# A linear-attention and gated-MLP kernel: W_in through the hardware DMA queue, a halved first step, W_spatial transposed by DMA, filler matmuls and a new order

## The chip, the cores and the metric

The kernel runs on one core of a Trainium2 chip. The core has a matrix engine (PE, or TensorE; the profile lists its weight loads apart, as PEld), three other compute engines (DVE or VectorE, ACT or ScalarE, POOL or GpSimd) and a sync engine (SP) that here only issues DMAs. The metric is the device time of one execution in microseconds. Three timed executions of the kernel before gave 152.79, 153.34 and 153.37 us; the median is 153.34 us.

## The reference

Two layers follow each other. All inputs are float32; the output is float32 of 4 x 768 x 512.

1. Linear attention with decay, for 4 batches, 8 heads, 768 tokens and a head size of 64, in blocks of 64 tokens. For each block: `intra = ((q k^T) * decay mask) v`, `inter = (q * decay) state`, `out = intra + inter`, and then `state = lam^64 * state + (k * decay)^T v`. The heads are laid side by side, so the layer gives x of 768 x 512 per batch.
2. A gated MLP: `h = relu(x W_in)`, with W_in 512 x 1024; u is the first half of h, v the second; v is normalised over its 512 features; `v_s = W_spatial v_n + b` mixes tokens with a 768 x 768 matrix; the output is `(u * v_s) W_out`, with W_out 512 x 512.

## The kernel before

**Steps.** The work is cut into 12 steps n of 256 tokens, three to a batch. Token 2p+m of a step lies on partition p, in column group m. A step has these operations, each named by a short token with its step number:

- loads of q, k and v of the step, LQ, LK, LV (512 KB each, line 184, into three buffers of each kind, so that load n overwrites what load n-3 brought);
- KC and QC, casts to bfloat16 (lines 266 to 274); VD, v times its decay (line 292);
- TK and TQ, 8 PE transposes each (line 300), with EK and EQ, their evictions from PSUM (EQ multiplies by the decay, line 313);
- SC, scores (line 329), MK, their mask (line 333), KV, the state update (line 345), SS, a copy of the state, AV, intra and inter (lines 366 and 375), EX, the eviction of x to the tile xT;
- PV and EV, the v half of h and its relu (lines 401 and 406), BN, RA, RD, VN, the statistics and the normalisation; PU and EU, the u half (line 439).

When a batch's three steps are done, PW multiplies by the transposed W_spatial (line 461; f counts four blocks of features, i two halves of the 768 tokens), GB adds b (line 466), GM multiplies by u (line 472), PO multiplies by W_out (line 478; one block t of 128 output tokens), EO evicts and ST stores. GM for half i = 0 serves the PO blocks t = 0 to 2, half i = 1 the blocks 3 to 5. For the last four steps (8 to 11) q is scaled by QM, and the transposes of q and k are made by DMA (DQ, DK) instead of by the PE.

**Weights.** W_in, W_spatial and W_out are loaded by POOL through the software DMA queue, which casts float32 to bfloat16 on the way (WI, WS, WO, lines 239 to 248). In front of each stands GT (line 235), a copy of one element of a named q, k or v buffer: POOL waits there until the load that last wrote this buffer has landed, so the weight is not requested earlier. W_spatial is transposed by the PE (WT, 72 matmuls, line 451) and evicted by DVE and ACT (EW). WT takes every second column, which brings the tokens into the order of the partitions; GM (line 472) then reads u with a stride to bring the result back to token order.

**Order.** The order is written out by hand in a string, `ORDER`. Each token is operation, numbers, engine (T for PE, A for ACT, D for DVE, P for POOL, S for SP). Every engine runs its own tokens strictly in this order, and waits where an input or a buffer is not ready; a DMA that must wait also holds back all that stands behind it on its queue. Dependences follow from the order of the tokens: an operation that reads a buffer waits for the last token before it that writes that buffer.

Of the kernel before, what the change touches and what calls it, by code (L numbers as in the profile page):

```python
# [16 lines left out]
LK.0.2.S lam.A msk.P LQ.0.2.S LK.1.2.S idn.P mkc.D LV.0.2.S LB.6.T pos.P LN.6.A LK.2.2.S LL.D KC.0.2.P LX.A  # L17
LQ.1.2.S TK.0.6.T LT.0.A QC.0.2.D LQ.2.2.S TQ.0.5.T EK.0.6.A EQ.0.5.D KC.1.2.A SC.0.0.0.T LV.1.2.S SC.0.1.2.T
LT.2.A MK.0.0.0.D TK.1.6.T VD.0.2.P EK.1.6.A MK.0.1.2.D LV.2.2.S LT.1.A AV.0.0.0.T LK.3.2.S KV.0.0.T SS.0.0.A
GT.1.1.P WI.0.P QC.1.2.D KV.0.1.T AV.0.1.0.T KC.2.2.A LQ.3.2.S GT.1.1.P WI.1.P TQ.1.6.T EX.0.1.1.A TK.2.5.T  # L20
EQ.1.6.D GT.1.2.P WS.1.P EX.0.0.0.A QC.2.2.D EK.2.5.A SC.1.0.2.T LQ.4.2.S GT.1.2.P WS.0.P SC.1.1.0.T
MK.1.0.2.D TQ.2.6.T SS.0.1.A VD.1.2.P EQ.2.6.D MK.1.1.0.D SC.2.0.2.T SC.2.1.4.T MK.2.0.2.D AV.1.0.0.T KV.1.0.T
LV.3.2.S MK.2.1.4.D SS.1.0.A KV.1.1.T VD.2.2.P AV.1.1.0.T SS.1.1.A PV.0.0.6.T EX.1.1.1.A EX.1.0.0.A PV.0.1.1.T
EV.0.0.6.A AV.2.0.2.T BN.0.0.D PV.1.1.6.T EV.0.1.1.D KV.2.0.T BN.0.1.D PV.1.0.5.T SS.2.0.A EV.1.1.6.D RA.0.A
AV.2.1.2.T BN.1.1.D PU.1.0.6.T BS.S EV.1.0.5.A RD.0.D PU.0.1.4.T VN.0.0.D EX.2.1.3.A KC.3.2.P BN.1.0.D
EX.2.0.2.A PU.1.1.5.T EU.0.1.4.A EU.1.0.6.D PV.2.0.3.T RA.1.A VN.0.1.D EU.1.1.5.A RD.1.D TK.3.6.T VN.1.1.D
EV.2.0.3.A PU.2.0.2.T VN.1.0.D EK.3.6.A BN.2.0.D PV.2.1.3.T EU.2.0.2.A PU.2.1.6.T EV.2.1.3.A LK.4.2.S WT.3.2.T
BN.2.1.D EU.2.1.6.A QC.3.2.P WT.4.3.T WT.0.5.T EW.3.2.D RA.2.A WT.1.6.T LK.5.2.S EW.4.3.D EW.0.5.A WT.5.4.T
WT.2.2.T RD.2.D VN.2.1.D EW.5.4.A TQ.3.3.T QC.4.2.P VN.2.0.D PU.0.0.5.T EW.2.2.A EQ.3.3.D LQ.6.2.S EW.1.6.A
TQ.4.4.T VD.3.2.P SC.3.1.0.T EU.0.0.5.A EQ.4.4.D SC.3.0.2.T PW.0.0.1.6.T LQ.5.2.S MK.3.1.0.D PW.0.1.1.5.T  # L30
GB.0.0.1.6.D LV.4.2.S MK.3.0.2.D PW.0.1.0.4.T GM.0.0.1.P KC.4.2.A PW.0.0.0.6.T GB.0.1.1.5.D GB.0.1.0.4.D
LK.6.2.S GM.0.1.1.P TK.4.5.T GB.0.0.0.6.D PW.0.2.1.4.T GM.0.1.0.P EK.4.5.D LK.7.2.S AV.3.0.0.T GT.0.5.P WO.P
GB.0.2.1.4.D SC.4.0.2.T SC.4.1.5.T KV.3.0.T MK.4.0.2.D PW.0.3.1.4.T GM.0.2.1.P SS.3.0.A LV.6.2.S QC.6.2.P
MK.4.1.5.D KV.3.1.T AV.3.1.0.T KC.5.2.A PW.0.3.0.3.T GM.0.0.0.P SS.3.1.D GB.0.3.1.4.D LV.5.2.S QC.5.2.A
TK.5.6.T EX.3.1.1.D GM.0.3.1.P PW.0.2.0.2.T GB.0.3.0.3.D EX.3.0.0.A VD.4.2.P EK.5.6.A GM.0.3.0.D TQ.5.3.T
GB.0.2.0.2.D PV.3.1.5.T EQ.5.3.D PU.3.0.6.T EV.3.1.5.A GM.0.2.0.P AV.4.0.0.T BN.3.1.D EU.3.0.6.A SC.5.1.2.T
SC.5.0.4.T LQ.8.2.S KV.4.0.T MK.5.1.2.D PV.3.0.6.T SS.4.0.A MK.5.0.4.D KV.4.1.T EV.3.0.6.A AV.4.1.0.T LK.8.2.S
KC.6.2.P PO.0.0.3.T EX.4.0.0.A BN.3.0.D EX.4.1.1.A PO.0.1.6.T EO.0.0.3.D RA.3.A LK.9.2.S PV.4.0.2.T RD.3.D
SS.4.1.D EO.0.1.6.A VN.3.1.D VD.6.2.P VN.3.0.D PV.4.1.3.T EV.4.0.2.A ST.0.0.S TK.6.6.T BN.4.0.D EV.4.1.3.A
PO.0.2.2.T EK.6.6.A BN.4.1.D VD.5.2.P TQ.6.3.T LV.9.2.S EO.0.2.2.A PU.3.1.5.T EQ.6.3.D RA.4.A PO.0.3.6.T  # L40
QM.8.0.D QM.8.1.P EU.3.1.5.A ST.0.1.S RD.4.D AV.5.0.0.T VN.4.1.D EO.0.3.6.A SC.6.0.2.T VN.4.0.D SC.6.1.4.T
KV.5.0.T MK.6.0.2.D PO.0.5.6.T SS.5.0.A KC.7.2.P ST.0.3.S AV.5.1.0.T MK.6.1.4.D LQ.11.2.S TK.7.3.T EX.5.1.1.A
PU.4.0.2.T EX.5.0.0.A EK.7.3.A PV.5.1.5.T LK.10.2.S EU.4.0.2.A PV.5.0.4.T ST.0.2.S EV.5.1.5.A LQ.7.2.S
PU.5.1.3.T EO.0.5.6.A BN.5.1.D EV.5.0.4.A PO.0.4.6.T EU.5.1.3.A BN.5.0.D ST.0.5.S PU.5.0.2.T EO.0.4.6.A
LV.8.2.S RA.5.A PU.4.1.3.T EU.5.0.2.A RD.5.D VN.5.0.D AV.6.0.0.T VN.5.1.D EU.4.1.3.A KV.6.0.T ST.0.4.S
PW.1.0.0.6.T SS.6.0.A PW.1.0.1.5.T GB.1.0.0.6.D LQ.9.2.S GM.1.0.0.P PW.1.1.0.6.T GB.1.0.1.5.D LV.7.2.S
QC.7.2.D GM.1.0.1.P KV.6.1.T AV.6.1.0.T GB.1.1.0.6.D KC.8.2.A PW.1.2.0.5.T EX.6.0.0.D DQ.8.S GM.1.1.0.P
EX.6.1.1.A SS.6.1.D PW.1.2.1.6.T DK.8.S GB.1.2.0.5.D VD.8.2.P PW.1.3.0.5.T GB.1.2.1.6.D LK.11.2.S PU.6.0.6.T
GB.1.3.0.5.D GM.1.2.0.P TQ.7.4.T GM.1.3.0.D EU.6.0.6.A GM.1.2.1.P PU.6.1.5.T EQ.7.4.D LV.11.2.S QM.9.0.P
PO.1.0.6.T EU.6.1.5.A SC.7.0.0.T VD.7.2.P EO.1.0.6.A SC.7.1.2.T PO.1.2.5.T MK.7.0.0.D LQ.10.2.S PV.6.1.6.T  # L50
MK.7.1.2.D QM.9.1.P PO.1.1.4.T LV.10.2.S EV.6.1.6.A EO.1.2.5.D AV.7.0.0.T BN.6.1.D EO.1.1.4.A SC.8.1.2.T
SC.8.0.5.T KV.7.0.T MK.8.1.2.D PV.6.0.4.T ST.1.1.S SS.7.0.A KV.7.1.T MK.8.0.5.D EV.6.0.4.A AV.7.1.0.T
PW.1.1.1.3.T SS.7.1.A ST.1.0.S VD.9.2.P EX.7.1.1.D AV.8.0.4.T EX.7.0.0.D GB.1.1.1.3.D KV.8.0.T DQ.9.S
PU.7.1.6.T KC.9.2.D SS.8.0.A GM.1.1.1.P KC.10.2.A BN.6.0.D AV.8.1.4.T QM.10.1.P PV.7.0.3.T EU.7.1.6.A DK.9.S
QM.10.0.D EX.8.0.4.A DK.10.S PV.7.1.6.T RA.6.A VD.10.2.P EV.7.0.3.A RD.6.D VN.6.1.D DQ.10.S EX.8.1.5.A
PW.1.3.1.2.T BN.7.0.D PV.8.1.3.T EV.7.1.6.D GB.1.3.1.2.D PV.8.0.6.T ST.1.2.S EV.8.1.3.A BN.7.1.D GM.1.3.1.P
PU.7.0.2.T EV.8.0.6.A BN.8.1.D QM.11.0.P RA.7.A PO.1.3.3.T BN.8.0.D EU.7.0.2.A QM.11.1.P PO.1.5.6.T VN.6.0.D
EO.1.3.3.A RD.7.D RA.8.A VN.7.1.D SC.9.0.0.T ST.1.3.S EO.1.5.6.A SC.9.1.2.T VN.7.0.D PO.1.4.5.T MK.9.1.2.D
ST.1.5.S PU.8.1.6.T EO.1.4.5.A RD.8.D MK.9.0.0.D PU.8.0.4.T ST.1.4.S EU.8.1.6.A VN.8.0.D AV.9.0.0.T EU.8.0.4.A
VN.8.1.D SC.10.1.2.T SC.10.0.5.T KV.9.0.T MK.10.1.2.D PW.2.0.0.4.T SS.9.0.A MK.10.0.5.D KV.9.1.T AV.9.1.0.T  # L60
KC.11.2.A PW.2.1.0.3.T DQ.11.S VD.11.2.P GB.2.0.0.4.D SS.9.1.D EX.9.0.0.A DK.11.S PW.2.1.1.6.T GB.2.1.0.3.D
EX.9.1.1.A PV.9.0.5.T GM.2.0.0.P GB.2.1.1.6.D PU.9.1.4.T GM.2.1.1.P EV.9.0.5.A PV.9.1.6.T BN.9.0.D GM.2.1.0.P
EU.9.1.4.A PW.2.3.1.5.T EV.9.1.6.A BN.9.1.D PW.2.3.0.6.T GB.2.3.1.5.D RA.9.A AV.10.0.0.T GB.2.3.0.6.D
GM.2.3.1.P SC.11.0.2.T SC.11.1.4.T RD.9.D KV.10.0.T MK.11.0.2.D PU.9.0.6.T SS.10.0.A VN.9.1.D KV.10.1.T
# [12 lines left out]
"""


@with_exitstack  # L80
def kernel(
    ctx: ExitStack,
    tc: tile.TileContext,
    q: bass.AP,
    k: bass.AP,
    v: bass.AP,
    lam: bass.AP,
    moe_w_in: bass.AP,
# [6 lines left out]
    P = 128  # L95
# [158 lines left out]
    def ld_k(e, n, x):  # L254
        load(k, k_in, n, *hx(x), e)
# [47 lines left out]
    def t_k(e, n, b):  # L303
        tr(n, b, kc)
# [230 lines left out]
```

## Time and profile before

| | |
|---|---|
| median of the timed runs | 153.34 us |
| time of the profiled execution | 152.98 us |
| its span, first to last instruction | 151.2 us |
| PE busy | 133.6 us, 88% |
| DVE / ACT / POOL busy | 106.9 / 81.4 / 75.6 us |
| DMA | 30.73 MB, mean 203 GB/s |

The profile is one execution. A busy time is a sum over instructions, a span is a time on the clock; the busy shares of the engines overlap. Durations of single matmuls overlap each other, so the time that a group of matmuls takes is read from the chain of work that ended last, where each piece has the time that it added. "x8" behind a piece is its number of instructions.

### The profile page before, as it was taken

The numbers are of one execution on the slowest core, as the hardware profiler recorded it, in microseconds if no ns is written. First come the engines' busy times: TensorE is split into PE (matmuls) and PEld (weight loads), VectorE is DVE, ScalarE is ACT, GpSimd is POOL, SyncE is SP. The second block draws the span as 40 slices with busy tenths as digits, with TensorE's granted clock in tenths as the row PEclk, the third lists the DMA queues.
The fourth block names the chain that finished last, engine by engine and source line by source line (L and its number), as shares of the span: only waits on it lengthen the run. The fifth ranks groups of instructions, "written<-read, shape, count | busy, mean of one in ns | idle before, by whom it ended". The sixth has DMA issues, their size and how long they took to land.

```text
span 151.2 us, 4756 instructions
## 1 busy us (share of the span) xinstructions
PE 133.6 (88%) x2026; PEld 87.2 (58%) x2026; DVE 106.9 (71%) x190; ACT 81.4 (54%) x146; POOL 75.6 (50%) x74
## 2 busy tenths in 40 slices
PE   1274947999999989977999999999999999999990
PEld 1264844677766754645766756556657655666540
DVE  1454593986999998685747799999958981936701
ACT  3987815698623837737724434765553344831161
POOL 7425980203669922780039975990293240016520
PEclk9999999999999999999999999999999999999999
DMA  3999999999988998999999799994170003121255
GB/s 108 300 290 290 283 216 216 217 248 304 281 221 237 172 301 216 269 310 342 319 341 276 142 306 311 202 208 177 41 138 4 2 4 139 57 81 72 74 219 197
DMA packets 52040, 30.73 MB, mean 203 GB/s; under 512 B 9522, under 2 KB 48946, under 8 KB 52018
## 3 DMA queue, kind: packets, MB, share of 16 engines
q1 hardware_dynamic: 49488, 27.53, 71.0%
q0 software_dynamic: 2384, 2.75, 10.6%
q8 instruction: 16, 0.26, 0.7%
q10 hardware_dynamic: 146, 0.13, 0.3%
q14 instruction: 6, 0.05, 0.1%
HBM read 24.77 MB, written 6.29 MB: 205 GB/s over the span
## 4 chain that ended last, share of the span: by engine, by line
PE 70%; DMA 16%; DVE 5%; SPq 4%; issue 2%; POOL 0%; ACT 0%; ACTq 0%
PE ps L461 20%; PE ps L439 13%; PE ps L401 13%; PE ps L478 11%; DMA q_in<-in_q_dram 10%; DMA win_sb<-in_moe_w_in_dram 6%; SPq L184 4%; PE ps L375 3%; PE ps L345 3%; PE ps L329 3%; PE ps L300 2%; PE ps L366 2%; PE ps L451 1%; DVE vsb L466 1%; DVE vn L430 1%
## 5 line engine op out<-in xcount | busy, mean ns | idle before, releaser
L472 POOL TENSOR_TENSOR gT<-vsb,uT 128x384 bf16<-128x384 f32 x27 | 30.1, 1128 | 33.6 <-DVE vsb L466 33.3
L461 PE MATMUL ps<-wt_sb,vn 128*128 128x384 bf16 x192 | 33.9, 327 | 0.0
L292 POOL TENSOR_TENSOR vd<-v_in,lv 128x1024 bf16<-128x1024 f32 x12 | 22.8, 1905 | 17.1 <-issue 6.4
L333 DVE TENSOR_TENSOR a_sb<-ps,m 128x1024 bf16<-128x1024 f32 x24 | 28.4, 1214 | 1.8 <-PE ps L329 1.6
L416 DVE BATCH_NORM_STATS2 st<-vh 128x6 f32<-128x512 bf16 x24 | 16.5, 688 | 11.9 <-ACT vh L406 11.7
L461 PEld LDWEIGHTS <-vn 128*128 128x128 bf16 x192 | 17.9, 98 | 11.9
L401 PE MATMUL ps<-win_sb,xT 128*128 128x512 bf16 x96 | 23.6, 380 | 0.8 <-DMA win_sb<-in_moe_w_in_dram 0.8
L439 PE MATMUL ps<-xT,win_sb 128*128 128x256 bf16 x192 | 24.1, 273 | 0.0
L478 PE MATMUL ps<-wout_sb,gT 128*128 128x512 bf16 x96 | 23.4, 380 | 0.0
L466 DVE TENSOR_TENSOR vsb<-ps,bsp 128x384 f32<-128x384 f32 x32 | 17.6, 552 | 6.8 <-PE ps L461 5.4
L439 PEld LDWEIGHTS <-win_sb 128*128 128x128 bf16 x192 | 18.3, 98 | 4.4
L168 ACT ACTIVATE o_sb<-ps 128x512 f32<-128x512 f32 (+1 forms) x21 | 12.3, 586 | 14.9 <-PE ps L478 10.7
L406 ACT ACTIVATE vh<-ps 128x512 bf16<-128x512 f32 x21 | 12.5, 597 | 13.6 <-PE ps L401 13.6
L406 ACT ACTIVATE uT<-ps 128x512 bf16<-128x512 f32 x22 | 13.2, 598 | 6.9 <-PE ps L439 6.7
L401 PEld LDWEIGHTS <-xT 128*128 128x128 bf16 x96 | 8.8, 98 | 9.6 <-issue 0.8
L478 PEld LDWEIGHTS <-gT 128*128 128x128 bf16 x96 | 9.0, 98 | 8.8
L168 ACT ACTIVATE s_sb<-ps 128x256 bf16<-128x256 f32 x14 | 5.3, 381 | 16.1 <-PE ps L345 16.1
L430 DVE TENSOR_SCALAR vn<-vh,mv,rstd 128x512 bf16<-128x512 bf16 x24 | 12.5, 551 | 0.3
L375 PE MATMUL ps<-a_sb,vd 64*64 64x128 bf16 x384 | 11.1, 225 | 1.7 <-DVE a_sb L333 1.0
L168 ACT ACTIVATE kc<-k_in 128x1024 bf16<-128x1024 f32 x7 | 7.4, 1056 | 8.4 <-PE ps L345 5.1
L168 ACT ACTIVATE xT<-ps 128x512 bf16<-128x512 f32 x19 | 10.5, 591 | 1.4 <-PE ps L375 1.3
L329 PE MATMUL ps<-qT,kT 64*64 64x128 bf16 x384 | 8.4, 233 | 2.5 <-DVE qT L313 2.5
(64 smaller groups left out, 155.6 us busy)
## 6 DMA issues: line engine op xcount, KB each, us to landing
k_in<-in_k_dram SPq DMA_DIRECT2D x12, 512.0 KB, 7.3
q_in<-in_q_dram SPq DMA_DIRECT2D x12, 512.0 KB, 7.3
v_in<-in_v_dram SPq DMA_DIRECT2D x12, 512.0 KB, 7.1
out_dram<-o_sb SPq DMA_DIRECT2D x23, 256.0 KB, 2.5
wsp_raw<-in_moe_w_spatial_dram POOLq DMA_DIRECT2D x2, 576.0 KB, 16.1
win_sb<-in_moe_w_in_dram POOLq DMA_DIRECT2D x2, 512.0 KB, 10.6
wout_sb<-in_moe_w_out_dram POOLq DMA_DIRECT2D x1, 512.0 KB, 10.7
bsp<-in_moe_b_spatial_dram SPq DMA_DIRECT2D x1, 384.0 KB, 8.1
```

The costliest lines, as they stand in the source:

```text
L168: nc.scalar.activation(out=o, in_=i, func=AF.Copy)
L292: vec(e).tensor_tensor(out=vd[n % NCA][:, h], in0=v_in[n % NIN][:, h], in1=lv[:, n % NR, h].unsqueeze(3).broadcast_to((P, h.stop - h.start ...
L333: nc.vector.tensor_tensor(out=a_sb[n % NA][:, i].rearrange("p o w j x -> p (o w) (j x)"), in0=bank(b, 2).rearrange("p o (w y) -> p (o w) y ...
L375: nc.tensor.matmul(out=po[row(w), c ^ o, c, i], lhsT=vd[n % NCA][row(c), 4 * o + u, j, :], rhs=a[row(c), i, o, w, j, :], start=(r == 0 and ...
L401: nc.tensor.matmul(out=bank(b), lhsT=x[:, c, g], rhs=win_sb[:, g, DH:DFF], start=(g == 0), stop=(g == NCH - 1))
L406: nc.scalar.activation(out=o, in_=i, func=AF.Relu)
L416: nc.vector.bn_stats(out=st6[p2][:, t], in_=vh[p2][:, t])
L439: nc.tensor.matmul(out=pu[:, f2].rearrange("p (c x) -> p c x", c=2), lhsT=win_sb[:, g, f * P:(f + 1) * P], rhs=x[:, :, g, :], start=(g == ...
L461: nc.tensor.matmul(out=bank(b)[:, 0:HW], lhsT=vn[bb % 2][:, s, f * P:(f + 1) * P], rhs=wt_sb[:, s, i * HW:(i + 1) * HW], start=(s == 0), s ...
L466: nc.vector.tensor_tensor(out=vsb[(bb * 4 + f) % NVS][:, i * HW:(i + 1) * HW], in0=bank(b)[:, 0:HW], in1=bsp[:, i * HW:(i + 1) * HW], op=A ...
L472: vec(e).tensor_tensor(out=gT[bb % 2][:, f, cols].rearrange("p (a y m) -> p a y m", m=2, y=Q64), in0=vsb[(bb * 4 + f) % NVS][:, cols].rear ...
L478: nc.tensor.matmul(out=bank(b), lhsT=gT[bb % 2][:, f, t * P:(t + 1) * P], rhs=wout_sb[:, f, :], start=(f == 0), stop=(f == NCH - 1))
```

## The change

- **W_in** is loaded in float32 by SP, through the hardware queue: WI.0 (the v half, 1 MB) into the output buffer o_sb, which is idle then and is now one tile, WI.1 (the u half) into a new tile wst. New operations WC cast it, one of four row blocks each (two on ACT, two on DVE, four on POOL).
- **Step 0** is loaded, cast, transposed and scored in halves of four heads each; a half is two DMAs of 128 KB. VD works in halves in all steps.
- **W_spatial** stays on the software queue, but is transposed by six DMAs on SP (DW, each a block of 128 x 768, SBUF to SBUF). WT and EW go. The token order is now set where AV writes PSUM (a strided output), and GM reads and writes contiguous rows.
- **Fillers**: WU issues matmuls of 128 x 128 on a constant, 136 in all, 105 of them ahead of the first PV.
- VN runs on ACT for 16 of its 24 tiles (as `rstd * v - mean * rstd`, so RD makes a second small tile, nmr). SY, a copy of two elements, stands in front of nine EX pairs. Step 8's q and k are transposed by the PE again; DQ and DK remain for steps 9 to 11.
- **A new order.** The whole string is new. On SP it begins Q0 and K0 in halves, Q1, K1, V0 in halves, V1, WI.0, Q2, K2, WI.1, V2, K3, Q3, V3, K4, Q4, K5, V4, Q5, Q6, b, V5, DW.0, DW.1, DW.2, K6, Q7, V6, K7, DW.4, DW.3, DW.5, V7, ST.0.2, Q8. On POOL it holds ... VD.3.1, VD.3.0, GT.2.0, WS.0, KC.5, VD.4.1, VD.4.0, QC.5, VD.5.0, GT.2.2, WS.1, GT.0.3, WO, GM.0.1.0, KC.6, GM.0.3.0, QC.7, GM.0.2.0. On the PE, the four PW of batch 0 with i = 0 stand behind all of steps 0 to 4, and the first PO behind all of step 5.

```diff
-LK.0.2.S lam.A msk.P LQ.0.2.S LK.1.2.S idn.P mkc.D LV.0.2.S LB.6.T pos.P LN.6.A LK.2.2.S LL.D KC.0.2.P LX.A
...
+LQ.0.1.S lam.A pos.P LK.0.1.S LQ.0.0.S LK.0.0.S msk.P WU.-8.T LB.1.T LQ.1.2.S LN.1.A LL.D idn.P LK.1.2.S
+QC.0.1.A LX.A LV.0.1.S KC.0.1.D WU.15.T TQ.0.1.2.T LT.0.A TK.0.1.0.T LV.0.0.S QC.0.0.D WU.4.T TQ.0.0.6.T
...
+SC.5.1.3.T BN.3.0.D LK.6.2.S SC.5.0.1.T PV.4.1.5.T EU.4.1.6.A MK.5.0.1.D VD.5.0.P VN.1.0.A LQ.7.2.S PU.3.0.0.T
+VD.5.1.D EV.4.1.5.A GT.2.2.P WS.1.P PU.4.0.6.T VN.2.1.A MK.5.1.3.D LV.6.2.S GT.0.3.P WO.P TQ.6.1.T EU.4.0.6.A
...
     def load(src, dst, n, x, e):
+        if x == 2:
+            eng.dma_start(out=dst[n % NIN].rearrange("p h m d -> p h (m d)"),
+                          in_=src[b, :, t].rearrange("h (p m) d -> p h (m d)", m=2))
+        else:
+            for h in (2 * x, 4 + 2 * x):
+                eng.dma_start(out=dst[n % NIN][:, h:h + 2].rearrange("p h m d -> p h (m d)"),
+                              in_=src[b, h:h + 2, t].rearrange("h (p m) d -> p h (m d)", m=2))
...
+    def w_u(e, n):
+        if n < 0:
+            nc.vector.memset(warm, 1.0)
+        for x in range(abs(n)):
+            nc.tensor.matmul(out=bank(SB)[:, 4 * D:4 * D + P], lhsT=warm, rhs=warm, start=(n < 0 and x == 0), stop=True,
+                             skip_group_check=True)
...
     def after(e, x, n):
-        nc.gpsimd.tensor_copy(out=seen, in_=(k_in, q_in, v_in)[x][n % NIN][0:1, 0, 0, 0:1])
+        nc.gpsimd.tensor_copy(out=seen[:, 0:1], in_=(k_in, q_in, v_in)[x][n % NIN][0:1, H - 1, 0, 0:1])
 
     def w_in(e, j):
         f = slice(DH, DFF) if j == 0 else slice(0, DH)
-        nc.gpsimd.dma_start(out=win_sb[:, :, f],
-                            in_=moe_w_in.rearrange("(g p) f -> p g f", p=P)[:, :, f])
+        nc.sync.dma_start(out=stage(j), in_=moe_w_in.rearrange("(g p) f -> p g f", p=P)[:, :, f])
+
+    def stage(j):
+        return o_sb[:, 0:NCH] if j == 0 else wst
+
+    def w_c(e, j, g):
+        f = slice(DH, DFF) if j == 0 else slice(0, DH)
+        copy(e, win_sb[:, g, f], stage(j)[:, g])
...
     def a_v(e, n, part, b):
-        po = bank(b, 2).rearrange("p z (c i x) -> p z c i x", c=2, i=2)
+        po = bank(b, 2).rearrange("p z (c i y m) -> p z c i m y", c=2, i=2, m=2)
...
+    def s_y(e, n, b):
+        copy(e, seen, ps[0:1, b:b + 2, 0:1].rearrange("p z x -> p (z x)"))
...
     def v_n(e, n, c):
         t, p2 = 2 * (n % NR) + c, n // NR % 2
+        if e == "A":
+            nc.scalar.activation(out=vn[p2][:, t], in_=vh[p2][:, t], func=AF.Identity,
+                                 scale=rstd[p2][:, t:t + 1], bias=nmr[p2][:, t:t + 1])
+            return
...
-    def w_t(e, s, b):
-        pw = bank(b).bitcast(BF16)
-        for a in range(NT):
-            for m in range(2):
-                nc.tensor.transpose(out=pw[row(m), a * P:(a + 1) * P], in_=wsp_raw[:, a, s * P + m:(s + 1) * P:2],
-                                    identity=ident)
-
-    def e_w(e, s, b):
-        pw = bank(b).bitcast(BF16)[:, 0:S]
-        copy(e, wt_sb[:, s], pw)
+    def d_w(e, a):
+        nc.sync.dma_start_transpose(wt_sb[:, :, a * P:(a + 1) * P], wsp_raw[:, a])
...
-        vec(e).tensor_tensor(out=gT[bb % 2][:, f, cols].rearrange("p (a y m) -> p a y m", m=2, y=Q64),
-                             in0=vsb[(bb * 4 + f) % NVS][:, cols].rearrange("p (a y m) -> p a y m", m=2, y=Q64),
-                             in1=uT[bb % 2][:, f, cols].rearrange("p (a m y) -> p a y m", m=2, y=Q64), op=ALU.mult)
+        vec(e).tensor_tensor(out=gT[bb % 2][:, f, cols], in0=vsb[(bb * 4 + f) % NVS][:, cols],
+                             in1=uT[bb % 2][:, f, cols], op=ALU.mult)
```

## The prediction

> **What bounds the kernel now.** I read the busy time by stage first, with cuts where the chain of work changes hands: the first PV (24.00), the first PW (40.25), the first PO (57.13), the end of the last PE wait (69.30), the last matmul (147.50). Columns: stretch, its length, busy time of PE, PEld, DVE, ACT, POOL, granted clock, DMA share, GB/s.
>
> ```profile
> 0.00:24.00 24.00, 12.67 (x299) 10.67 (x300) 12.70 (x19) 16.16 (x30) 14.72 (x24) 1.00 1.08 246
> 24.00:40.25 16.25, 16.25 (x265) 11.61 (x264) 12.07 (x28) 12.37 (x22) 4.18 (x4) 1.00 1.13 252
> 40.25:57.13 16.88, 16.15 (x312) 10.70 (x305) 16.32 (x22) 7.08 (x11) 12.07 (x12) 1.00 0.99 238
> 57.13:69.30 12.17, 10.34 (x160) 6.30 (x158) 9.74 (x19) 7.35 (x14) 7.29 (x5) 1.00 1.03 273
> 69.30:147.50 78.20, 78.20 (x1007) 47.95 (x1004) 55.67 (x104) 38.01 (x70) 37.30 (x30) 1.00 0.63 162
> ```
>
> From 69.30 on the PE never stops. Ahead of that the DMA is full, and the PE waits for data. The chain that ended last (start, duration, what) names the waits:
>
> ```profile
> 14.00 0.65 POOL seen L235
> 14.65 9.29 DMA win_sb<-in_moe_w_in_dram
> 23.94 0.04 issue
> 23.98 1.89 PE ps L401 x8
> ...
> 57.49 7.18 DMA q_in<-in_q_dram
> 64.67 0.02 issue
> 64.69 0.88 DVE qc L277
> ...
> 67.67 1.14 DVE a_sb L333
> 68.81 0.04 issue
> 68.85 0.61 PE ps L300 x8
> ...
> 142.33 5.19 PE ps L478 x24
> ```
>
> W_in is asked for only at 14.65 and the PE gets it at 23.94. A late q load, then a full DVE, hold the PE before 68.85. The queues and weight loads, from the page (queue: packets, MB, share of 16 engines; load: count, KB, median us from issue to landing):
>
> ```profile
> q1 hardware_dynamic: 49488, 27.53, 71.0%
> q0 software_dynamic: 2384, 2.75, 10.6%
> ...
> wsp_raw<-in_moe_w_spatial_dram POOLq DMA_DIRECT2D x2, 576.0 KB, 16.1
> win_sb<-in_moe_w_in_dram POOLq DMA_DIRECT2D x2, 512.0 KB, 10.6
> wout_sb<-in_moe_w_out_dram POOLq DMA_DIRECT2D x1, 512.0 KB, 10.7
> ```
>
> So the time is: when does the PE become saturated, and how much work has it left then.
>
> **The PE's work.** Prices from the chain, per token: PV and PO 0.865 (x8 in 1.73), PU 0.87, PW 1.01, a pair of SC 0.50, AV 0.46 (0.22 where a batch begins), KV 0.24, TK and TQ 0.45, all WT 2.13. Counted over the PE's tokens: 125.2 before, 124.0 after (WT goes; step 8's two transposes come, 0.9). Check: from 69.30 to 147.50 these prices give 77.1 for 78.2, so a remainder is multiplied by 1.014. Behind the last matmul lie 3.7 of span (the same halves EH and SH stay), and 1.8 outside the span (152.98 against 151.2). In the new order the work ahead of a token is: first PV 5.7, first PU 10.5, KV.3.0 16.6, KV.4.0 23.0, TQ.5 27.0, KV.5.0 32.8, first PW 33.5, first PO 42.3.
>
> **When data lands.** Loads before landed at 4.9, 6.7, 8.5, 10.4, 12.2, 14.0, 15.8: 1.8 per 512 KB while the hardware queue is alone. Step 0's eight half DMAs are issue-bound (0.5 each on SP against 0.45 of transfer): K0 lands at 7.1 instead of 6.7. Then Q1 8.9, K1 10.7, V0 12.5, V1 14.3. W_in's 1 MB halves have no row: at the rate of these loads 3.6; the best slice of the page, 342 GB/s, mixes loads with stores whose rows are 2 KB as W_in's are, and if stores were half of it they ran at 415 GB/s, 2.5. I take 2.8, nearer the rows of equal length. So WI.0 17.1, Q2 18.9, K2 20.7, WI.1 23.5, V2 25.3, K3 27.1, Q3 28.9, V3 30.7, K4 32.5, Q4 34.3, K5 36.1, V4 37.9.
>
> WS.0 stands on POOL behind VD.3 (two halves at about 1.0; a full VD is 1.9, and a 512-element QM 1.05 in the median), so it is issued at 32.9. Software loads landed 9.3 (the first W_in) to 17.5 after issue, the long ones behind others; alone I take 10: 42.9. It also takes engine time from the hardware queue: 10.6% of 151.2 is 16.0 for 2.75 MB, so 3.4 for its 0.59 MB. Hence Q5 43.1, Q6 44.9, b 46.3, V5 48.1.
>
> **The walk, part by part.**
>
> *Start.* PV.0.0 needs WI.0 and a cast (half of a 1.04 POOL cast, 0.53): 17.7. The PE is there at about 18.0, after VD.1 (16.3) and AV.1. Before it was 23.98, with 1.4 more of step 2 done. The 105 fillers ahead of PV.0.0 (0.056 each when transposes run at x8 in 0.45, so 5.9) lie in PE waits for step 0 and 1's loads; uncovered they would cost those 5.9. SP loses nothing: WI is issued while the queue is full anyway.
>
> *Second half of W_in.* WI.1 at 23.5 and three POOL casts in a row: PU.0.0 at 25.1 (W 10.5). WC on DVE, ACT (0.35 to 0.6 each) delay EQ.2 and QC.2, which wait for step 2's loads longer.
>
> *Steps 2 to 4.* KV.3.0: 25.1 + 6.1 + 0.8 for 15 fillers is 32.0, VD.3 is ready at 32.7. KV.4.0: 39.1, VD.4 ready at 39.9. TQ.5: 43.9, QC.5 ready at 44.1. KV.5.0 at 49.9; VD.5 was ready at 49.1.
>
> *W_spatial by DMA.* DW.0 waits on SP for WS.0 (42.9). K6, Q7, V6 and K7 queue behind it. A transpose of 128x1024 held SP for 1.24 to 2.77 and landed after 3.1 to 4.0; a block has three quarters of that. Price of one block in the queue: from 0.9 to 3.6; I take 1.2, three quarters of the median issue (1.6). Behind V5: 48.1 + 3.6 = 51.7. The PE reaches the first PW at 50.6 and waits 1.1. EW's 3.9 of ACT and DVE goes.
>
> *W_out.* GT.0.3 reads a k buffer whose last writer in the new order is K6, no longer K3. K6 lands at 53.5, POOL holds WO until then, and GM.0.1.0, KC.6 and QC.7 behind it. WO is issued at 53.7 and lands 9.3 to 11.9 later. I take 9.3: SP stands at DW.4 for WS.1 (49.3 + 10), so the hardware queue runs dry. That is 63.0. The PE reaches the first PO at 51.7 + 8.8 = 60.5 and waits 2.5.
>
> *Rest.* DW.3 to 5 are done near 63 + 1, and V7, ST.0.2, Q8 behind them by 70; their users stand 8 or more later (PW.0.0.1 at 63.0 + 5.9, TQ.8 at 79). No wait counted.
>
> *Costed at nothing.* VN on ACT: 16 of about 0.6, 9.6 on an engine with 70 idle; DVE loses 8.8 of its 106.9, and it was full from 40 to 57. Identity is not in the trace: if it needed table loads (1.28 each, up to two for each of 12 RA), 30 of ACT, which at 54% would still be beside PE mostly; I take 0. AV's strided output: nearest row is WT's strided weight load, 110 ns against 98; from 0 to a doubling of AV, 10; I take 0, and below nothing is excluded since the matmuls are the same. GM contiguous: DVE 1.22 to perhaps 0.55 (the row of GB), five of them, not on the path after 69. SY: 9 of 0.1 to 0.2. POOL: about 3 more of VD and WC in halves against 75.6.
>
> **Sum.** 63.0 + 1.014 x 81.7 (82.8) + 3.7 + 1.8 = 151.3, against 152.98: minus 1.7. On the median of 153.34 that is 151.6; I say 151.5.
>
> **A rule against the row.** Moving W_in between queues is spoken against by the Trainium skill, "DMA: Bandwidth & Descriptors", section "Issuing engines are not separate DMA queues": DMAs of all issuers run on the same 16 engines, and another issuer saves only issue time. The trace agrees on the sharing: K3 took 14.6 to land beside the software loads, 7.3 is the usual. By that rule alone W_in costs the same 7.2 for 2 MB at the loads' rate and the sum would be 1.6 later; what I count is its earlier request, not bandwidth. The same page, "Latency and other measured facts", has DMA transposes at 261 GB/s: 0.75 for a block, an estimate, so WO and the sum would be 1.4 earlier. No run here shows that rate.
>
> **The rivals.**
>
> *A, the weights are hidden (0.27).* GT.0.3 or the transposes cost less, and the first PO starts when the PE gets there without either wait: 59.4. Then 59.4 + 82.8 + 3.7 + 1.8 + 0.36 (to the median) = 148.1. For it: W_out before landed at 56.7, just ahead of its PO. Against it: K6 behind three transposes.
>
> *B, slower: the transposes clog SP's queue (0.25).* One mechanism: DW blocks cost more than 1.2. At 2.4, K6 and so WO are 3.6 later: 155.2; at 3.6 it is 158.8. It decides when W_out lands after 64.7, that is at 1.8 per block. For it: landings of 3.1 to 4.0 each, a median SP hold of 1.76 for qT. Against it: that row has full-size transposes and several waits on other work.
>
> *C, no net change (0.08).* W_in ahead of steps 2 to 5 only moves the wait: DMA is full to 69 either way, and the 6 gained at the first PV are lost to later loads. 153.3.
>
> *Forecast (0.40):* its own range 150 to 153.
>
> **Numbers.** The measurement can tell about 0.5% (0.8 us) from no change. Faster: A and four fifths of the forecast, 0.59. Same: C and 0.05 of the forecast, 0.13. Slower: B and what is left, 0.28. The range of 8 in 10 runs from 146.5 (A with the KV waits gone too) to 157.0 (B at 3 per block).
>
> **What would show it.** Right: first PV (matmul group of win_sb with xT) near 18, first PU near 25, first PW near 52, a PE wait at the first PO that ends with the DMA of wout_sb near 63, no PE wait after 70; POOL's `seen` ended by k_in near 53. Wrong: the PE waiting for wt_sb for many us (B), no wait at the first PO (A), DVE or ACT as releaser of PE waits between 30 and 60, AV pieces longer than 0.46, or ACT table loads beside the first three.

## The result and the profile after

The changed kernel takes 158.99 us (median of four runs, 157.34 to 159.53) against 153.3 us for the kernel before on the same chip: a ratio of 1.036, 95% interval 1.028 to 1.044. The forecast was 151.5, a gain, in a range from 146.5 to 157.0; the kernel became slower instead. The profiled execution after took 159.53 us; its span is 157.8 (before: 152.98 and 151.2). Ratios, here and below, leave out executions that are more than 1.5% above the fastest of the same kernel, and medians do not, so where the two disagree both are given.

The parts of the page after that answer to those shown of before: busy time (share of the span, instructions), the granted TensorE clock in 40 slices, the queues (packets, MB, share of 16 DMA engines) and the share of the chain that ended last by engine.

```profile
span 157.8 us, 4968 instructions
PE 148.6 (94%) x2106; PEld 100.5 (64%) x2106; DVE 98.6 (62%) x191; ACT 92.7 (59%) x171; POOL 68.5 (43%) x83
PEclk9999995999999999999999999999999999999998
q1 hardware_dynamic: 53376, 30.28, 77.5%
q0 software_dynamic: 1328, 1.70, 6.1%
PE 87%; DMA 5%; SPq 3%; ACT 2%; issue 1%; DVE 0%; ACTq 0%; DVEq 0%
```

TensorE (PE) is busy for 148.6 us, 15.0 more than before (133.6), though the count of work tokens says that it has 1.2 us less to do. The chain that ended last is PE for 87% (before: 70%), DMA for only 5% (before: 16%). So the waits that the change was to remove did go, and the time came out longer: the work itself has become dearer. The fillers are in the 15.0 (136 of them, busy 13.4 in the modelled ends; those ahead of the first PV lie mostly where the PE would have stood idle, as run e3 below shows). The rest is found by setting the same pieces of the chain (start, duration, what) beside each other. First before, then after:

```profile
25.87 0.24 PE ps L366 x8
26.11 0.22 PE ps L375 x16
```

```profile
34.37 0.34 PE ps L414 x8
34.72 0.44 PE ps L423 x16
```

These are the two kinds of matmul of AV (L366 and L414: q with the state; L375 and L423: the masked scores with v). The reader is to see that 16 matmuls of the same shape take 0.44 in place of 0.22, and 8 take 0.34 in place of 0.24. The group in the page says it again, busy time and mean ns behind the bar, before and after:

```profile
L375 PE MATMUL ps<-a_sb,vd 64*64 64x128 bf16 x384 | 11.1, 225 | 1.7 <-DVE a_sb L333 1.0
```

```profile
L423 PE MATMUL ps<-a_sb,vd 64*64 64x128 bf16 x384 | 16.1, 310 | 0.0
```

The stretches by 1 us of the kernel after (columns as in the prediction) show a second, small loss: the PE stands for most of 23 to 24 with no releaser, and then runs at half clock for 3.4 us, over its first PV.

```profile
22.00:23.00 1.00, 0.77 (x36) 0.66 (x24) 0.00 (x0) 0.97 (x2) 0.41 (x1) 1.00 1.02 373
23.00:24.00 1.00, 0.12 (x4) 0.13 (x4) 0.00 (x0) 0.23 (x1) 0.63 (x1) 0.96 1.06 367
24.00:25.00 1.00, 1.00 (x7) 0.39 (x6) 0.00 (x0) 0.00 (x0) 0.00 (x0) 0.50 1.17 311
25.00:26.00 1.00, 1.00 (x5) 0.45 (x4) 0.00 (x0) 0.00 (x0) 0.00 (x0) 0.50 1.21 295
26.00:27.00 1.00, 1.00 (x13) 1.00 (x11) 0.00 (x0) 0.96 (x2) 0.91 (x2) 0.50 1.23 286
27.00:28.00 1.00, 1.00 (x9) 0.65 (x8) 0.42 (x1) 0.41 (x2) 0.82 (x3) 0.83 1.13 281
```

From the stop at 22.8 to the end there is no PE wait above 0.2, none for W_out among them, although the rest of the forecast's chain is in place (K6 landed at 55.3, W_out was issued at 55.73 and landed at 64.9): the PE, slowed by AV, reaches the first PO only at 68.78. In the other three executions of this kernel the mean granted clock was 0.995 to 1.00 (0.987 in this one), and they took 157.34 to 159.09, so the half clock does not explain the loss.

### The profile page after: what moved, and what is told of

The parts are those of the page before. It is cut to its first block, busy times and chain, and to the rows that moved or that the text cites. A ratio compares the mean times of both kernels' runs of the same rounds, so it can differ in the third digit from the quotient of the medians.

```text
span 157.8 us, 4968 instructions
## 1 busy us (share of the span) xinstructions
PE 148.6 (94%) x2106; PEld 100.5 (64%) x2106; DVE 98.6 (62%) x191; ACT 92.7 (59%) x171; POOL 68.5 (43%) x83
## 4 chain that ended last, share of the span: by engine, by line
PE 87%; DMA 5%; SPq 3%; ACT 2%; issue 1%; DVE 0%; ACTq 0%; DVEq 0%
PE ps L512 20%; PE ps L452 14%; PE ps L498 14%; PE ps L528 13%; PE ps L423 7%; PE ps L336 5%; DMA k_in<-in_k_dram 5%; PE ps L414 4%; PE ps L377 4%; PE ps L393 3%; PE ps L214 3%; SPq L197 2%; ACT kc L176 1%; ACT s_sb L176 0%; SPq L193 0%
## 5 line engine op out<-in xcount | busy, mean ns | idle before, releaser
L523 POOL TENSOR_TENSOR gT<-vsb,uT 128x384 bf16<-128x384 f32 x27 | 24.4, 912 | 43.0 <-DVE vsb L517 42.8
L322 POOL TENSOR_TENSOR vd<-v_in,lv 128x512 bf16<-128x512 f32 x23 | 23.9, 1055 | 9.3 <-DMA v_in<-in_v_dram 7.6
L452 PE MATMUL ps<-win_sb,xT 128*128 128x512 bf16 x96 | 25.3, 391 | 0.0
L423 PE MATMUL ps<-a_sb,vd 64*64 64x128 bf16 x384 | 16.1, 310 | 0.0
L176 ACT ACTIVATE xT<-ps 128x512 bf16<-128x512 f32 x21 | 11.8, 595 | 7.0 <-PE ps L423 7.0
L214 PE MATMUL ps<-warm 128*128 128x128 bf16 x136 | 13.4, 255 | 2.1 <-DVE warm L212 1.1
L457 ACT ACTIVATE uT<-ps 128x512 bf16<-128x512 f32 x20 | 11.9, 593 | 4.3 <-PE ps L498 4.3
L486 ACT ACTIVATE vn<-vh,nmr,rstd 128x512 bf16<-128x512 bf16 x16 | 12.9, 812 | 2.5 <-DVE nmr L480 2.5
L362 DVE TENSOR_TENSOR qT<-ps,lq 128x1024 bf16<-128x1024 bf16 (+1 forms) x10 | 6.4, 636 | 12.7 <-ACT s_sb L176 7.5
L214 PEld LDWEIGHTS <-warm 128*128 128x128 bf16 x136 | 10.7, 116 | 4.0 <-issue 1.9
## 6 DMA issues: line engine op xcount, KB each, us to landing
wst<-in_moe_w_in_dram SPq DMA_DIRECT2D x1, 1024.0 KB, 10.7
```

The lines of the kernel that those rows point to most:

```text
L176: nc.scalar.activation(out=o, in_=i, func=AF.Copy)
L214: nc.tensor.matmul(out=bank(SB)[:, 4 * D:4 * D + P], lhsT=warm, rhs=warm, start=(n < 0 and x == 0), stop=True, skip_group_check=True)
L322: vec(e).tensor_tensor(out=vd[n % NCA].rearrange("p (o i w) m d -> p o i (w m) d", o=2, i=2)[o], in0=v_in[n % NIN].rearrange("p (o i w) m ...
L423: nc.tensor.matmul(out=po[row(w), c ^ o, c, i], lhsT=vd[n % NCA][row(c), 4 * o + u, j, :], rhs=a[row(c), i, o, w, j, :].rearrange("p (m y) ...
L452: nc.tensor.matmul(out=bank(b), lhsT=x[:, c, g], rhs=win_sb[:, g, DH:DFF], start=(g == 0), stop=(g == NCH - 1))
L457: nc.scalar.activation(out=o, in_=i, func=AF.Relu)
```

## The experiments

The theory after this profile (W): AV writes PSUM with a stride of two columns in the new form, so that the output comes out in token order, and such a matmul runs at half rate. Its rivals: the permuted form costs by itself, wherever the permutation stands; the fillers are the loss; the forecast's mechanism B, the transposes on SP, is the loss.

**e1, one part undone: AV writes contiguously.**

```
-        po = bank(b, 2).rearrange("p z (c i y m) -> p z c i m y", c=2, i=2, m=2)
+        po = bank(b, 2).rearrange("p z (c i x) -> p z c i x", c=2, i=2)
...
-            rhs=a[row(c), i, o, w, j, :].rearrange("p (m y) -> p m y", m=2),
+            rhs=a[row(c), i, o, w, j, :],
```

> The changed kernel with one edit undone: AV writes its PSUM output in contiguous columns again. The order of the tokens is then not restored anywhere, so the output is not the reference's; every instruction and byte stays. Theory W (the strided PSUM write makes the AV matmuls twice as slow, and the PE never waits after 24 us, so each us of AV is a us of time): AV's intra part goes from 0.44 back to 0.22 and its inter part from 0.34 to 0.24, so 24 x 0.32 = 7.7 less, 151 to 152 us. Theory S (the AV groups look longer only because something else holds the PE, and the loss is the late start): AV groups stay long or the time moves less than 2 us, 157 to 159 us.

Measured: 154.2 us, ratio 1.0115 (1.0056 to 1.0174), so below the kernel after by 4.8 us by the medians and by 3.8 us (2.5%) by the ratios, which hold each kernel against the one before on its own chip. AV's pieces are back at 0.24 and 0.22. And with the PE earlier, the chain that the prediction had drawn comes to light, step for step (pieces under 0.1 are left out):

```profile
26.57 7.00 DMA v_in<-in_v_dram
33.73 2.05 POOL vd L322 x2
35.84 7.91 DMA wsp_raw<-in_moe_w_spatial_dram
43.77 2.73 SPq L507
46.56 2.78 SPq L507
49.39 1.28 SPq L507
50.71 4.87 DMA k_in<-in_k_dram
55.71 0.17 POOL seen L255
56.16 9.57 DMA wout_sb<-in_moe_w_out_dram
65.77 2.76 PE ps L528 x12
```

V3, its VD on POOL, W_spatial, three transposes on SP, K6, the copy that holds W_out back, W_out, first PO. The PE waits 1.7 for it. So the strided AV is most of the loss (2.5% of 3.6%), and under it lies a second bound.

**e4, the one part alone, in the kernel before.** The reverse edit of L354 and L376 of the kernel before: AV's write is strided there, all else stays (tokens come out ordered twice).

> The kernel before with one edit of the change alone: AV writes PSUM with the stride. The tokens are then ordered twice, so the output is not the reference's. Theory W: 24 AV cost 0.32 more each, of which the ones after 24 us (20) and most of the PE-bound rest count: 6 to 7.5 more, 159 to 161 us. Theory S: no change, 153 us.

Measured: 162.86 us, ratio 1.0667 (1.0619 to 1.0714): 10.2 us more. The pieces change as in the kernel after (L366 0.34 for 8, L375 0.44 for 16); 24 times 0.22 and 20 times 0.10 make 7.3 of it, and the granted clock, 0.76 in the mean from 24 to 40 us of the profiled execution (half from 21.6 to 31.8), up to 3.8. All four executions have the same mean clock, 0.968. The reading that the stride costs only in company of the other edits falls.

**e2, the permutation moved to the moving operand.** AV writes contiguously and reads q and the scores with the halves of a row interleaved, so the result is in token order as in the kernel after.

```
-    rhs=qv(n, o, u, c),
+    rhs=qv(n, o, u, c).rearrange("p m y -> p y m"),
...
-    rhs=a[row(c), i, o, w, j, :].rearrange("p (m y) -> p m y", m=2),
+    rhs=a[row(c), i, o, w, j, :].rearrange("p (m y) -> p y m", m=2),
```

> The changed kernel, but the token order is set by reading the moving operand of AV with a stride (64 elements) and writing contiguous columns; it computes the reference. Theory W (it is the write into PSUM): AV falls to 0.22 and 0.24 as in the run with contiguous output, 151 to 152 us. Rival V (any strided operand of the matmul costs the same): AV stays at 0.44 and 0.34, 158 to 159 us.

Measured: 158.59 us, ratio 1.038 (1.0323 to 1.0436), the same as after; the AV matmuls in the chain average 34 ns (L423) and 48 ns (L414), no better than with the strided write (29 and 42). So "only the write" was too narrow: reading the moving operand out of sequence costs the same.

**e5, the permutation moved to the eviction.** AV contiguous on both sides; EX, which copies PSUM to xT on ACT and DVE anyway, reads PSUM in token order.

```
-        src = bank(b).rearrange("p (c i x) -> p c i x", c=2, i=2)
+        src = bank(b).rearrange("p (c i m y) -> p c i y m", c=2, i=2, m=2)
...
-        copy(e, dst, src)
+        copy(e, dst.rearrange("p a i (y m) -> p a i y m", m=2), src)
```

> The changed kernel with the token order moved once more: AV writes contiguous columns, and EX, the eviction, reads PSUM with the stride of 64. It computes the reference. Theory W (it is the matmul's access pattern that costs, 0.32 for each AV): AV at 0.22 and 0.24, the time of the run with contiguous output, 153 to 155 us, with a PE wait of 1 to 2 us for wout_sb at the first PO. Rival E (a strided read of PSUM costs ACT and DVE as much as the PE): EX doubles from 0.6 to 1.2, 24 times, and the AV gain is lost, 157 to 159 us.

Measured: 153.66 us, ratio 1.0152 (1.011 to 1.0195). EX did not become dearer (578 to 606 ns on ACT for a piece of 128x512, 672 to 692 on DVE; before it was 577 to 615 and 677 to 682), AV's pieces are the short ones. So the order that the new GM wants is to be had for nothing here, and what is left of the loss is not AV. Against the kernel after, its profiled execution (span 152.4) can be cut into stretches:

| stretch | after | e5 |
|---|---|---|
| start to first PV | 24.12 | 23.80 |
| first PV to first PO | 44.66 | 43.22 |
| first PO to the end of the last matmul | 85.40 | 81.75 |
| last matmul to the end | 3.6 | 3.6 |

In the third stretch the chain holds nothing but PE work on both sides. AV's pieces add up to 8.43 us there after (190 matmuls of L423, 71 of L414) and to 4.84 here (191 and 76): 3.59 of the 3.65 between the two. In the second stretch AV costs the kernel after some 2.8 more, and its half clock up to 1.7, while this one waits 1.9 for W_out and 0.4 for the copy SY.

**e3, no fillers, in the kernel after.** All 136 WU matmuls go.

> The changed kernel without its 136 filler matmuls. Theory F (the fillers are on the path: they hold 5.0 us of the chain, they use up the PE's instructions so that a fetch stalls it for 1.1 at 22.8, and the clock then falls to 0.5 for 3 us, 1.6): up to 7.7 less, 151 to 155 us, first PV near 21. Rival C (the fillers lie in waits and keep the clock up): no gain, groups before the first PV at half speed (8 transposes in 1.0), first PV at 24 or later, 158 to 161 us.

Measured: 156.21 us, ratio 1.0238 (1.0174 to 1.0302), faster than after by 2.8 us by the medians and 1.9 by the ratios, whose intervals overlap. The PE waits that they filled come back (for lam_in 2.1, for qc 2.0, for kc 2.0), and yet the first PV is no later, 23.99. They did do something ahead of it. The same transposes of step 1 (start, duration, what), with the fillers and without:

```profile
12.05 0.62 PE L336 MATMUL ps<-ident,qc 128*128 128x128 bf16 x8 [0.80 <-POOL qc L180]
```

```profile
11.26 1.04 PE L336 MATMUL ps<-ident,qc 128*128 128x128 bf16 x8 [0.55 <-POOL qc L180]
```

The PE runs at half speed without them. The page of e3 prints a granted clock of 0.998, but the profile has no record of it before 23.70 there (before 10.27 in the kernel after). So a PE at full speed from 10 us on gained nothing at the first PV: rival C was right that the fillers keep the clock up, and wrong that this is worth time; theory F's first PV near 21 did not come either. What they cost lies behind the first PV, where the stretch to the first PO fell from 44.66 to 40.93 in the profiled executions: in the kernel after 31 fillers stand there in the chain for 2.4, and its half clock costs up to 1.7.

**e8, fillers that write every second column, in the kernel after.**

```
-  nc.tensor.matmul(out=bank(SB)[:, 4 * D:4 * D + P], lhsT=warm, rhs=warm, ...
+  nc.tensor.matmul(out=bank(SB)[:, 4 * D:4 * D + 2 * P:2], lhsT=warm, rhs=warm, ...
```

> The changed kernel with the fillers writing every second column of PSUM, on the full 128 x 128 array, with contiguous operands; nothing else. This measures the disputed price alone. Theory W (a PSUM write with a stride of two columns runs at half speed): eight fillers in a row, 0.61 with the wait, and 0.056 each when warm, become about 0.11 each; time 2 to 5 us more. Rival Q (it is the small 64 x 64 tiles that suffer): fillers stay at 0.056 and the time at 158 to 160 us.

One run: 159.43 us. Pieces of the chain at full clock, the kernel after first, this one second:

```profile
31.53 0.22 PE ps L214 x4
```

```profile
30.44 0.44 PE ps L214 x4
```

55 ns become 110 for a 128 by 128 matmul of 128 columns: the rate halves on the full array too, not only on 64 by 64 tiles. The time hardly moves: most of the fillers lie in waits, and this one execution has neither the stop at 22.8 nor the half clock of the kernel after, which hides what the 31 behind the first PV add (1.7 by their price).

**e6, W_out without the copy that holds it back.** On e5, `GT.0.3.P` goes, so POOL issues W_out without waiting for K6.

> As the run with EX reordering, and without GT.0.3, so that W_out is requested right behind the second half of W_spatial and not once K6 has landed. Theory K (the prediction's chain V3, WS.0, three transposes, K6, W_out sets the first PO once AV is cheap): W_out is issued at 52 and not at 56, lands near 62, no PE wait at the first PO, 1.5 to 2 us less than with GT.0.3. Rival D (the earlier W_out takes DMA time from K6, Q7, V6 and W_spatial, whose waits take over): the same time within 0.5 us.

Measured: ratio 0.9982 (0.9922 to 1.0041), against 1.0152 with the copy: about 1.7%, 2.6 us. The medians of ten executions each do not show it (153.98 against 153.66), and the ratio rests on four of this kernel's ten, so the gain in time is not certain. What the profile shows is that the wait went: W_out took 12.3 us to land instead of 9.9, and was there in time, with no PE wait at the first PO (65.51, in e5 67.02).

**e7, the same without fillers.**

> As the run without GT.0.3, and without the 136 fillers. Theory F (fillers ahead of and between the first PVs are on the path, about 2.5 us as their removal from the changed kernel gave): 2 to 3 us less, 149 to 151 us, faster than the kernel before. Rival D (data bounds the start and the first PO then): less than 1 us, with PE waits for DMA between 60 and 75.

Measured: 152.67 us, ratio 0.9988 (0.9946 to 1.003); no different from the one with fillers, so theory F misses. In its profiled execution (155.23) the PE has lost 3.6 us to two waits that end in nothing the profile shows (1.5 and 2.1), and 4.2 to Q1 and the identity.

**e9, the halves undone.** On e7, Q0, K0, Q1, K1, V0, V1 as whole loads.

```
-LQ.0.1.S lam.A pos.P LK.0.1.S LQ.0.0.S LK.0.0.S msk.P ... LV.0.1.S ... LV.0.0.S
+LQ.0.2.S lam.A pos.P LK.0.2.S msk.P ... LV.0.2.S
```

> The kernel with contiguous AV writes, the reordering in EX, W_out without the copy of K6 and no fillers (e7_wo_early_no_fill), with one change: step 0's inputs are loaded whole again, Q0 K0 Q1 K1 V0 V1 in that order, so that SP issues 6 transfers where it issued 12. Theory H (the halves delay step 1): in e7 nine issues of 0.45 to 0.47 stand before K1, which is issued at 4.9 and lands at 12.5; with whole loads it is issued near 2.4 and lands by 10.5, the wait of TensorE for qc of step 1 (2.2) goes, the first PV runs 1.5 to 2 earlier than 24.3, and the time is 1 to 2 below e7 (150.7 to 151.7). Rival B (the bytes ahead of K1, 2 MB, set its landing, not the issues): K1 lands within 0.7 of 12.5, the first transposes start 1.5 to 2 later, the time is that of e7 within 0.7. Rival S (the halves are worth what the change says): first SC from 9.0 to 10.5 or later, first PV later than 24.8, time 0.7 or more above e7.

Measured: 151.92 us, ratio 0.9986 (0.9934 to 1.0038). K1's cast starts at 10.70 where it started at 12.47, and the first PV at 22.53 where it was 24.34: theory H is right about K1, and rivals B and S fall. How much of the 1.8 at the first PV is due to it is open, since e10, with the halves, has it at 22.99. The time is not to be told from e7's ratio, so the 1 to 2 us are not shown. The profiled execution, the fastest of ten (150.55), lies below H's range, the median above it.

**e10, W_in back on the software queue,** on e7; the casts on chip go.

> e7_wo_early_no_fill with W_in back on the software queue, cast by the transfer, and the 8 casts on chip gone; both halves issued by POOL where the change has SP issue them. Theory N (in this kernel W_in by either road is there before TensorE needs it: in e7 the weights are cast at 21.8 and the first PV runs at 24.3): first PV within 0.7 of 24.3, time within 0.7 of e7 (152.0 to 153.4), the DMA engines' busy share lower by about 1 point; a wait for win_sb of at most 0.8, as the kernel before has it. Rival R (the hardware road is worth something): a wait for win_sb of 1.5 or more ahead of the first PV or PU, time above 153.7. Rival I (the 1 MB transfers of W_in as f32 are what holds TensorE's instruction fetch up): the waits of 1.5 and 2.1 with no releaser go or fall under 0.7 in sum, and the time falls by 1.5 or more.

Measured: 153.31 us, ratio 1.0063 (1.0012 to 1.0114). First PV at 22.99, earlier than theory N said, and no PE wait for W_in at all. N holds in what matters: W_in is there in time by either road. Between this ratio and e7's lie 0.75%, with intervals that overlap, so the hardware road is worth about 1 us by the ratios and 0.6 by the medians (153.31 against 152.67), and neither is clear of the noise. The two waits without a releaser shrank to 0.8 and 0.6, which is not what rival I wanted, and the time did not fall.

**e11, an attempt at the best start,** on e7: K0, Q0, K1, Q1, V0, V1 whole, the tables on ACT ahead of the first cast of Q.

> e7_wo_early_no_fill with step 0's inputs whole and in the order K0 Q0 K1 Q1 V0 V1, TensorE's order K0 before Q0, LX and the first LT ahead of the first cast of Q on ACT (that cast goes to POOL). An attempt at a version that beats both kernels. Theory H (the start is bound by the issues and the order of the first loads): K1 lands near 9 as in the kernel before (its cast began at 8.6 there), Q1 near 10.7, first PV 2 to 3 earlier than 24.3, time 149.5 to 151.0, faster than before by 1 to 2%. Rival B (by the bytes; then the wait for Q1, K1 and V0 only changes places): first PV within 0.8 of 24.3, time 152 to 153.3, no different from before. Rival D (an earlier start is taken back by the chain of transfers V3, W_spatial, its transposes, W_out and V6, which is not moved by it): first PV 2 earlier, but PE waits of 1 to 2 at 40 to 70 us, time 151.5 to 153.

Measured: 152.39 us, ratio 1.005 (1.001 to 1.009). First PV 23.01, and W_out was waited for again (1.1). A miss: the first PV is 1.3 earlier than in e7 where I expected 2 to 3 (Q1's cast ended a PE wait only at 11.54), and rival D's wait is there.

**e12, step 8's K and Q transposed by DMA,** as the kernel before has it, on e9.

> e9_whole_first_loads with K and Q of step 8 transposed by DMA again, as the kernel before has them: TensorE loses 16 transposes (0.90 us by its rows, 0.45 for each of TK and TQ), their two evictions go, POOL and DVE multiply Q by the table in place of ACT's cast, and SP issues two more DMA transposes behind the load of Q of step 11. Theory P (from 23 us TensorE is the bound, so its work is the time): time 0.6 to 1.0 below e9, about 151.0, and faster than before by about 1%. Rival T (the two DMA transposes hold up what is behind them on SP, the loads of V9 to V11 and K11, and what they read is late): PE waits of 0.5 or more between 85 and 115 us, time as e9's or above it. Rival U (POOL, which takes half of the multiplication, is late with vd and gT): a wait of PE for vd or gT of 0.5 or more, time as e9's.

Measured: 159.45 us, ratio 1.0369 (1.0297 to 1.0441). A clear miss, mostly by rival T's mechanism though in another place: on SP the two transposes stood behind loads that hold SP for 1.6 to 2.1 each, and the PE waited for kT itself. The PE's waits, then the stretches behind the wait:

```profile
PE ps L377 <- DMA kT<-kc: 4.6, 1, 4.6
```

```profile
92.00:94.00 2.00, 0.34 (x16) 0.34 (x20) 0.00 (x0) 0.00 (x0) 1.07 (x2) 0.54 0.82 246
94.00:96.00 2.00, 2.00 (x47) 1.39 (x40) 1.58 (x3) 0.00 (x0) 2.00 (x3) 0.50 1.05 298
96.00:98.00 2.00, 2.00 (x6) 0.67 (x5) 1.11 (x1) 0.00 (x0) 2.00 (x3) 0.50 1.14 331
98.00:100.00 2.00, 2.00 (x22) 0.95 (x22) 0.00 (x0) 0.00 (x0) 1.71 (x2) 0.75 1.03 244
```

4.6 of wait, 1.3 more for vd ahead of it, and half clock from the end of the wait at 93.7 to about 99.0 (2.7 lost) are 8.6, less 0.9 of transposes saved: 7.7. Between the medians of e12 and e9 lie 7.5 us, between the ratios 5.8, and between the two profiled executions 10.0 (160.51 is the slowest of e12's six), of which two more stops of 0.6 and 0.5 are part. The wait of 1.3 for vd is what rival U named, so U has a share beside T.

No version beat the kernel before by more than the measurement can tell: the best three stand at 0.998 to 0.999.

## Why the prediction was wrong

**The step that failed** is the one under "Costed at nothing": "AV's strided output: nearest row is WT's strided weight load, 110 ns against 98; from 0 to a doubling of AV, 10; I take 0". The upper end was right and the choice was wrong. Measured in the chain, after against e5: 29 ns for 16 and 42 for 24 a matmul, 0.78 for an AV of 0.46; 3.8 (by the ratios) to 4.8 us (by the medians) in the first experiment, 10.2 in the kernel before, of which 7.3 are AV at full clock. Of the 7.5 us between the forecast and 158.99, e5, the same kernel with the short AV, leaves 2.2 (153.66); they belong to W_out, below. The row I chose by was a strided weight load, which reads SBUF into the array; the edit strides the write to PSUM and nothing in the trace before did that. Two ends ten microseconds apart, in a stage where the PE never stops, should have stood in the forecast as a rival of its own, and did not; "AV pieces longer than 0.46" stood only in the list of signs. The Trainium skill has the rule, which I had not weighed: the page "PSUM — Partial Sum Buffer", section "Specifications (TRN2)", gives PSUM lines of 8 bytes and says that any non-contiguous access pattern slows matmuls significantly. The runs agree and give it a size: a stride of two columns of f32 is 55 to 110 ns on the full array and 0.22 to 0.44 for 16 of the 64 by 64 matmuls.

**The rest of the walk,** against three executions (the last, e9, is the fastest of its ten; DW is the time of three blocks on SP):

| step | predicted | after | e5 | e9 |
|---|---|---|---|---|
| K1's cast can start | 10.7 | 12.70 | 12.74 | 10.70 |
| first PV | 18.0 | 24.12 | 23.80 | 22.53 |
| first PU | 25.1 | 31.59 | 29.72 | 28.81 |
| first DW starts (W_spatial landed) | 42.9 | 44.03 | 45.45 | 42.14 |
| DW.0 to 2 | 3.6 | 6.20 | 6.15 | 5.97 |
| first PW | 51.7 | 59.62 | 56.12 | 53.73 |
| first PO | 63.0 | 68.78 | 67.02 | 62.96 |
| end of the last matmul | 145.8 | 154.18 | 148.77 | 145.15 |

*Start: wrong by 6.* Before, the first PV was at 23.98, and it is at 24.12 after: the gain of the whole change is gone there. Of the 6.1, K1 is 2.0 (the halves do not land at the rate of whole loads; e9 gives it back). The larger part is not the data. In e9, with K1 at the forecast's 10.7, no fillers and a contiguous AV, the first PV is still 4.5 late. From K1 to it I had allowed 7.3; it took 11.8: cast (1.05), transposes, their eviction, the mask on DVE (1.24), KV, the state on ACT (0.39 twice, each a PE wait of 0.5), AV, one after the other. In these steps the PE waits for other engines, so a sum of PE prices is no walk. And 1.45 of it is a wait with no releaser. The PE's speed is a smaller part: in e9 it runs at half speed until 24.85 (8 transposes in 1.04), in e5 at full speed from 12.16, and e5 still takes 11.1 for these steps, 1.8 of it such a wait. The kernel before starts at half speed too (8 transposes in 1.03 at 6.06); the 1.00 that the prediction's row prints for 0 to 24 only says that the profile has no record of the clock there before 18.39.

*W_spatial by DMA: mis-sized.* A block held SP for 2.0 to 2.1 in these executions (6.0 to 6.2 for three; 6.9 in e1) where I took 1.2 in a range of 0.9 to 3.6. The estimate of 0.75 that stands beside it is further off. That is rival B's mechanism past its point of 1.8. At its scale, (2.07 - 1.2) x 3 = 2.6 later, 154.1: e5 measured 153.66, but that is partly luck. In e5 the third transpose left SP at 51.60, and the forecast had 51.7, because it let the blocks wait for V5 until 48.1 and they began at 45.45. What came later is K6: issued only then, it took 4.9 to land where I had 1.8, so W_out was issued at 57.11 and not at 53.7. Why K6 took so long is not shown. In the kernel after none of this shows in the time, because the PE is later still.

*W_out: right as a chain.* K6, the copy, POOL's issue and 9.2 to 9.9 of landing came in that order (with W_out there at 67.0 in e5 where I had 63.0); e1's chain shows every link, and taking the copy away took the wait away.

*The remainder: right.* I had 82.8 from first PO to the last matmul; with a contiguous AV it is 81.75 (e9: 82.2), with the strided one 85.40.

*At nothing, and right:* VN on ACT brought no table loads, though it runs at 0.81 and not 0.6; GM contiguous fell from 1.13 to 0.91 on POOL, off the path. *Fillers:* those ahead of PV were to lie in waits, and did; the 31 behind it are part of the 1.9 to 2.8 that taking all out gained in the kernel after.

*Rivals.* A (weights hidden) needed the early first PV and falls; its sign, no wait for W_out at the first PO, was there in the kernel after, but because the PE was late. C (the 6 at the start are lost again, 153.3) is nearest to what the change is without the strided AV, if for another reason: they were not there to lose.

**What stays open.** In e9 the stretch from first PV to first PO took 40.4 for 36.6 of counted work, 1% on top and 0.6 of waits; of the 2.7 left, about 1.2 is the half speed until 24.85, and some 1.5 are not traced. Nor is the scatter of ten runs over 3 us in the late kernels. What the wait without a releaser is, is only argued (below).

## What to carry to other kernels

Where an edit changes the access pattern of a matmul's output or moving operand, price it at up to twice the matmul until a row shows otherwise, and put the permutation into the eviction, which here read PSUM out of order at the same 0.6 us. Before filler matmuls or earlier weights are priced, follow the chain of other engines that the first tile hangs on: filling or feeding the PE did not shorten it here, nor did running it at full speed. A wait seen in the profile can hide the next: after AV was mended, the PE waited for W_out, and with that wait gone no single edit lowered the ratio any more.

## What the runs showed of the hardware

A stride of two f32 columns in PSUM halved a matmul's rate on the full array (110 ns for 55) and for the 16 matmuls of 64 by 64 (0.44 for 0.22); the 8 with the state went from 0.24 to 0.34. Reading the moving operand with neighbours 128 or 256 bytes apart cost as much (34 ns a matmul for 16, and 48 for 24).

In nine of the kernels the PE stopped once to three times for 0.5 to 2.1 us with no semaphore to wait for, first between 20 and 24 us. The PE's waits of e5 list it so:

```profile
PE ps L393 <- issue: 1.8, 1, 1.8
```

In the five of these waits that I followed, a 16 KB packet of the instruction queue had started 0.5 to 1.6 us before the stop and the PE went on 2.5 to 2.7 after the packet's start (packet and resumption: 21.20 and 23.88 in the kernel after, 21.16 and 23.61 in e5, 20.84 and 23.45 and again 44.84 and 47.37 in e7, 19.01 and 21.63 in e9). The other eight end 2.3 to 2.7 after such a packet too. It fits a PE that has run out of instructions while the DMA engines are full. Other such packets passed without a stop (19.96 in e3), and no run took the cause away, so this is argued, not shown.

The granted clock changes in steps of 3.41 us: every record of it that ends within a run is a whole number of them long (13.65 at full and 3.41 at half in the kernel after). It fell to half at 23.92 in the kernel after (for 3.41), at 24.44 in e6 (3.41), at 92.16 in e12, within its wait of 4.6 (6.83), and at 21.58 in e4 (10.24). In the 3.41 ahead of these falls the PE was busy for 1.83, 1.47, 0.30 and 1.29. Stops of 1.5 in e1, 1.8 in e5 and 2.1 in e7 left it at full; there the steps that hold the stop have 1.92 or more of busy PE. So the length of a stop alone does not tell, and where the border lies is open: a step of e5 with 1.76 (from 63.36) stayed at full as well. The fillers did not prevent the first fall.
